# K of eight tiles in one run a partition, products of their own for the memory keys, and another order of the opening

## The chip, the cores and the metric

The kernel runs on one core of a Trainium2 chip. The metric is the device time of one execution in microseconds (us). The engines are TensorE (PE; its weight load is listed as PEld), VectorE (DVE), ScalarE (ACT), GpSimd (POOL) and SyncE (SP); each works through its own list of instructions in order and waits there for semaphores of the others. SP only issues transfers here.

## The reference

Three stages, one after the other, on 4 x 768 = 3072 tokens of 512 features.

```
scores = scale * q_c @ concat(mem_k, k[c-16 : c+32+8])^T   # per head (8) and chunk of 32 queries: 8 + 56 keys
a      = exp(scores - max);  a = a / (sum(a) + 1e-9)
x      = a @ concat(mem_v, v[c-16 : c+32+8])
y      = softplus(x @ w_in) @ w_out                         # 512 -> 2048 -> 512
z      = leaky(y @ w_in2, alpha) @ w_out2                   # max(h,0) + alpha*min(h,0), 512 -> 2048 -> 512
```

## The kernel before, in words

Tokens are taken in 24 tiles of 128 (`QT`), four to a block of 512 (`TB`, six blocks). One tile's attention is a fixed row of pieces. SP loads q (2 transfers), K (`load_k`, one) and v (`load_v`, six). ACT puts q in order (`a_order`, two halves), POOL copies the eight memory keys beside both ends of K (`a_mem`), so that every chunk's 64 keys stand in one piece. PE makes the scores (`a_scores`: 16 products of 64 columns, called s0, s1, ... below), DVE takes the maximum (`a_max`), subtracts it (`a_shift`), ACT takes exp, DVE sums (`a_sum`) and inverts (`a_norm`), POOL (tiles 0 to 7) or DVE (later tiles) multiplies by the inverse (`a_share`), PE transposes (t0, t1, ...), ACT copies out (`a_turned`), PE multiplies with v (`a_values`: x0, x1, ...), ACT and DVE split the result into a high and a low part (`a_high`, `a_low`). The trace calls the buffers qk, v, ps_s, nm, sm, r, ps_t, pt, ps_x and x; later tiles keep q, K and the shares in qt, kt and s_sb.

The first MLP runs in 96 steps (`steps`, from `SEGMENTS`): step i makes one 128-wide slice of the hidden layer for one block in 12 products of 512 columns (h0, h1, ...; PSUM ps_hh), ACT takes softplus and the high part g, DVE the low part of g, and 12 more products (o0, o1, ...) add it to four output banks ps_o. Blocks 0 and 1 take turns: four slices each, four each, eight each; blocks 2 to 5 then take 16 slices in one go. At such a change of segment (o4, o8, o12, o16, ...) ACT and DVE must first copy the four banks out (o_sb). The weights come as 64-bit words ("raw", 0.5 MB each); DVE turns each into 32 bits with five instructions ("word"), ACT makes the high part and POOL the low part ("wsplit"). The second MLP (ps_q) follows.

The order on every engine is not written by hand. `schedule` gives each piece an engine, an estimated duration, the pieces it follows and a due time made of the step's time and a number from the table `O`; `Plan.run` takes, whenever an engine is free, the able piece with the earliest due time. Eight rounds feed the steps' times back, and the plan with the earliest end is issued piece by piece. All instructions pass one helper, so the trace has them all on line L71, and views go by buffer names. Where the plan sees PE idle, `keep_busy` sets products on a zeroed buffer ("zero") ahead of a piece. The first eight tiles keep q, K and v in rooms of the weight pool; tile 8 and the later ones have rooms of their own.

Of the kernel before, what the change touches and what calls it, by code (L numbers as in the profile page):

```python
# [13 lines left out]
B, H, S, D = 4, 8, 768, 64  # L14
# [68 lines left out]
RUNS = 8  # L83
O = {'qo': 19.43, 'km': 103.61, 's': 132.4, 'm': 86.98, 'c': -51.87, 'e': 175.6, 'n': -19.49, 'r': -46.35, 'w': -19.52, 't': 95.77, 'pt': 85.42, 'v': 4.11, 'xh': -85.13, 'xl': -37.52, 'first': 4.43, 'gap': 13.49, 'second': 13.8, 'gap2': 10.89, 'raw': 76.14, 'ab': -97.97, 'cl': -24.77, 'ca': -41.63, 'cb': -28.14, 'cc': -52.39, 'wh': 1.69, 'wl': -37.29, 'odd': 61.8, 'sp': 29.0, 'hi': -84.66, 'lo': 120.66, 'out': 14.22, 'wait': 0.06, 'sloads': 10.35, 'qo0': 31.77, 'qo1': 59.63, 'km0': 45.44, 'km1': -1.09, 's0': 33.53, 's1': 68.06, 'm0': 99.26, 'm1': -29.86, 'c0': 87.42, 'c1': 86.99, 'e0': -47.46, 'e1': 46.23, 'n0': 20.17, 'n1': -4.91, 'r0': 23.19, 'r1': -6.49, 'w0': -81.15, 'w1': -23.28, 't0': 107.79, 't1': -40.96, 'pt0': 0.74, 'pt1': -5.53, 'v0': -87.68, 'v1': 71.52, 'xh0': -18.53, 'xh1': -22.32, 'xl0': 2.53, 'xl1': 34.49, 'by0': 3.34, 'by1': 1.01, 'va': -80.0, 'vb': -248.8, 'vc': -188.24, 'vd': -121.62, 'ra': -92.44, 'rb': -99.39, 'rc': -59.46, 'wld': -3.93, 'dra': -16.84, 'qpd': -4.87, 'ca0': 0.43, 'ca1': -2.85}


class Plan:
# [16 lines left out]
    def run(self):  # L104
# [10 lines left out]
        while left:  # L115
# [61 lines left out]
def attention_mlp_mlp_kernel(ctx: ExitStack, tc, qk, v, w1, w2, consts, out):  # L177
# [178 lines left out]

    def load_v(t):
        for u, to, at, n in (
            (0, 0, MEM0, NMEM), (0, NMEM, 0, KW - NMEM), (0, KW, CHUNK, KW),
            (1, 0, 0, KW), (1, KW, SW - KW + NMEM, KW - NMEM), (1, 2 * KW - NMEM, MEM0 - D, NMEM),  # L360
        ):
            part = slice(u * DM, (u + 1) * DM)
            sp.dma_start(out=v_t[t][to:to + n, part], in_=v[t][at:at + n, part])

# [18 lines left out]
    def a_scores(t):  # L383

        ps = score_ps[t] = (ps_acc.tile([P, NPAIR, 2, KW], F32, tag="acc", name="ps_s") if t < TB
                            else ps_a.tile([P, NPAIR, 2, KW], F32, tag="pa", name="ps_s"))
        keep_busy(("s", t), ps.rearrange("p g u k -> p (g u k)"))
        for g in range(NPAIR):
            for j in range(NC):
                u, c = divmod(j, 2)  # L390
                n = 2 * (u * NPAIR + g)
                pe.matmul(
                    ps[c * D:(c + 1) * D, g, u, :], lhsT=q_t[t][:, c, n:n + 2, :].rearrange("p e k -> p (e k)"),
                    rhs=k_t[t][:, g, KEYS[j]:KEYS[j] + KW], start=True, stop=True,
                )

# [22 lines left out]

    def a_shifted_exp(t):  # L420
        _, s, nm, _ = st[t]
        x = score_ps.pop(t).rearrange("p g u k -> p (g u) k")
        for n in range(SLOTS):
            act.activation(out=s[:, n, :], in_=x[:, n, :], func=AF.Exp, bias=nm[:, n, :], scale=1.0 / float(D) ** 0.5)

# [481 lines left out]
    def schedule(when):  # L907
# [7 lines left out]

        def dma(name, issue, move, due, work, after=(), take=(), give=(), eng="SP"):
            add(("i",) + name, eng, issue, due, work, after, take)
            add(("x",) + name, "DMA", move, due, nothing, [("i",) + name])
            add(name, "", 2.0, due, nothing, [("x",) + name], [], give)

        for n, k in enumerate(order):
            f = k // 2
            need = when[first_use[f]] + (O["odd"] if k % 2 else 0)
            dma(("raw", n), 0.45, 1.9, (O["ra"], O["rb"], O["rc"])[n] if n < 3 else need - O["raw"], lambda k=k: load_raw(0, k), [("i", "raw", n - 1)] if n else [("i", "qk", TB - 1, 2)], ["raw"])
            add(("ab", n), "DVE", 0.45, need - O["ab"], lambda k=k: magnitude(0, k), [("raw", n)] + ([("ab", n - 1)] if n else []), ["word"])
# [9 lines left out]
        for i, (b, f, first, final) in enumerate(steps):  # L935
# [30 lines left out]
        def tile(t, prev, due, step=None):  # L966
# [10 lines left out]
            if not start:  # L977
                free_qk += [("s", TB - 1)]
            soon = -100 + 2 * t if start else due - O["sloads"]
            add(("qr", t), "", 0.0, soon, room, free_qk, qrooms)  # L980
# [6 lines left out]
            else:  # L987
                dma(("qk", t, 2), 1.45, 2.7, soon, lambda: (load(), load_k(t)), [("qr", t)])
# [4 lines left out]
            dma(("v", t), 2.9, 2.0, (O["va"], O["vb"], O["vc"], O["vd"])[t] if start else due - 24, lambda: load_v(t), [("vr", t)])  # L993
            queries = [("q", t, c) for c in range(2) if few or c]
# [9 lines left out]
            after_s = [("km", t)] + queries + ([("s", prev)] if prev >= 0 else []) + ([("t", TB - 1)] if t == TB else []) + ([("pt", prev)] if t > 2 * TB else []) + ([("h", step)] if step else [])  # L1004
            if t > 3 * TB:
# [4 lines left out]
            else:  # L1010
                add(("s", t), "PE", 1.2, due - when_due("s"), lambda: a_scores(t), after_s, [] if start else ["pa", "s"] if few else ["pa"], qrooms)
            add(("m", t), "DVE", 0.8, due - when_due("m"), lambda: a_max(t), [("s", t)])
            if not few and O["ca" + "01"[t >= TB]] > 0.5:
                add(("c", t), "DVE", 0.17, due - when_due("c"), lambda: a_bias(t), [("m", t)])
                add(("e", t), "ACT", 1.4, due - when_due("e"), lambda: a_shifted_exp(t), [("c", t)], [], [] if start else ["pa"], table="exp")
# [3 lines left out]
            add(("n", t), "DVE", 0.69, due - when_due("n"), lambda: a_sum(t), [("e", t)])  # L1019
            add(("r", t), "DVE", 0.40, due - when_due("r"), lambda: a_norm(t), [("n", t)])  # L1020
# [160 lines left out]
```

## Time and profile before

| | us |
|---|---|
| three runs | 1087.36, 1089.03, 1088.96 (median 1088.96) |
| the profiled execution, its whole time | 1090.53 |
| its span, first to last instruction | 1088.6 |
| PE busy in it | 1064.7 (98%) |
| DVE busy | 715.6 (66%) |
| ACT busy | 559.0 (51%) |
| POOL busy | 231.2 (21%) |

So PE stands still for some 24 us of the span. The views below tell where, and who holds it up. A row of the timeline gives the start, the duration, the engine, the operation, output<-input, and in brackets the idle time before it with what ended it; a row of the groups ("lines") gives how many, their busy time and the mean of one in ns.

### The profile page before, as it was taken

Reading aid. Unit: us, or ns where it says so; the run is one execution under the profiler, and the core shown is the slowest. Engines: PE = TensorE matmul, PEld = TensorE weight load, DVE = VectorE, ACT = ScalarE, POOL = GpSimd, SP = SyncE. Lnnn points to the kernel's source line nnn. Section 1 sums busy time; section 2 is a strip of 40 time slices with the busy share of each in tenths; the row PEclk is TensorE's granted clock in tenths of the full one; section 3 lists DMA queues with packets and bytes.
Section 4 is the critical chain, followed back from the end, with each engine's and each line's share of the span. In section 5 each row is a group of like instructions: output and inputs, shape, how many; then the busy total and the mean of one; then the engine's idle time right before and its main releaser. Section 6 shows DMA issues by size and latency. Waiting matters only on the chain.

```text
span 1088.6 us, 16448 instructions
## 1 busy us (share of the span) xinstructions
PE 1064.7 (98%) x5999; PEld 873.6 (80%) x6003; DVE 715.6 (66%) x1150; ACT 559.0 (51%) x974; POOL 231.2 (21%) x281
## 2 busy tenths in 40 slices
PE   6789999999999999999999999999999999999998
PEld 4578878888888888888888888888888888888886
DVE  6789989566744554454358156678666779566976
ACT  5654335565553554353244355664555755456643
POOL 4434434334222332223233400000000000000000
PEclk9999999999999999999999999999999999999999
DMA  9955574658644565444356373799874999856904
GB/s 227 226 154 173 170 190 129 172 170 207 173 143 155 158 188 139 171 123 145 107 201 229 132 289 125 283 280 323 199 278 174 329 299 256 251 209 251 377 1 78
DMA packets 173840, 214.55 MB, mean 197 GB/s; under 512 B 96064, under 2 KB 125888, under 8 KB 166848
## 3 DMA queue, kind: packets, MB, share of 16 engines
q1 hardware_dynamic: 169456, 196.59, 56.7%
q0 software_dynamic: 4032, 16.78, 7.8%
q8 instruction: 48, 0.79, 0.3%
q14 instruction: 32, 0.26, 0.1%
q10 hardware_dynamic: 272, 0.13, 0.0%
HBM read 154.74 MB, written 46.14 MB: 185 GB/s over the span
## 4 chain that ended last, share of the span: by engine, by line
PE 91%; DVE 3%; DMA 2%; issue 1%; SPq 1%; ACT 1%; POOL 0%; DVEq 0%; ACTq 0%; POOLq 0%
PE ps_q L71 42%; PE ps_o L71 23%; PE ps_hh L71 22%; DVE word L71 2%; PE ps_x L71 2%; PE ps_s L71 2%; DMA raw<-in_w_dram 1%; PE ps_t L71 1%; DMA qk<-in_qk_dram 1%; SPq L71 1%; DMA v<-in_v_dram 0%; ACT pt L71 0%; DVE sm L71 0%; DVE o_sb L71 0%; DVE g L71 0%
## 5 line engine op out<-in xcount | busy, mean ns | idle before, releaser
L71 PE MATMUL ps_hh<-x,wsplit 128*128 128x512 f32 x1152 | 281.1, 393 | 0.3 <-DVE x L71 0.2
L71 PE MATMUL ps_o<-g,wsplit 128*128 128x512 f32 x1152 | 279.1, 391 | 0.8 <-ACT ta L71 0.7
L71 PEld LDWEIGHTS ps_o<-g,wsplit 128*128 128x128 f32 x1152 | 214.8, 188 | 46.5 <-ACT ta L71 1.1
L71 PEld LDWEIGHTS ps_hh<-x,wsplit 128*128 128x128 f32 x1152 | 215.3, 189 | 45.5 <-DVE x L71 0.5
L71 PE MATMUL ps_q<-g,wout 128*128 128x512 f32 x1008 | 229.3, 389 | 0.0
L71 PE MATMUL ps_q<-xop,win 128*128 128x512 f32 x1008 | 229.1, 389 | 0.0
L71 PEld LDWEIGHTS ps_q<-g,wout 128*128 128x128 f32 x1008 | 189.0, 188 | 39.8 <-ACT gb L71 0.5
L71 PEld LDWEIGHTS ps_q<-xop,win 128*128 128x128 f32 x1008 | 189.2, 188 | 39.3
L71 DVE TENSOR_TENSOR g<-ta,g 128x512 fp32r<-128x512 f32 x96 | 71.2, 742 | 132.0 <-ACT g L71 131.8
L71 ACT CAST g<-gb 128x512 fp32r<-128x512 f32 x168 | 100.9, 622 | 89.6 <-PE ps_q L71 64.2
L71 DVE TENSOR_TENSOR g<-gb,g 128x512 fp32r<-128x512 f32 x168 | 114.0, 686 | 35.5 <-ACT g L71 33.6
L71 ACT CAST g<-ta 128x512 fp32r<-128x512 f32 x96 | 59.6, 621 | 147.5 <-PE ps_o L71 147.3
L71 ACT ACTIVATE ta<-ps_hh 128x512 f32<-128x512 f32 x96 | 57.4, 598 | 106.4 <-PE ps_hh L71 106.0
L71 DVE SCALAR_TENSOR_TENSOR word<-raw,word 128x512 int32<-128x512 int32 x128 | 104.6, 818 | 2.5
L71 ACT ACTIVATE tp<-gb 128x512 f32<-128x512 f32 x48 | 30.4, 633 | 91.8 <-DVE gb L71 91.8
L71 POOL TENSOR_TENSOR wst<-wsum,wst 128x512 fp32r<-128x512 f32 x32 | 42.1, 1316 | 122.4 <-ACT wst L71 122.3
L71 DVE TENSOR_SCALAR word<-word 128x512 f32<-128x512 f32 (+1 forms) x128 | 66.1, 521 | 1.8
L71 POOL DMA_DIRECT2D gb<-gb x12 | 10.5, 872 | 264.2 <-DVE g L71 183.0
L71 POOL TENSOR_TENSOR wsplit<-word,wsplit 128x512 fp32r<-128x512 f32 x32 | 48.9, 1530 | 64.4 <-ACT wsplit L71 64.2
L71 DVE TENSOR_SCALAR word<-raw 128x512 int32<-128x512 int32 x64 | 38.1, 597 | 36.8 <-DMA raw<-in_w_dram 23.8
L71 DVE SCALAR_TENSOR_TENSOR gb<-gb,tp 128x512 f32<-128x512 f32 x48 | 33.2, 691 | 44.0 <-ACT tp L71 44.0
L71 POOL TENSOR_TENSOR wst<-word,wst 128x512 fp32r<-128x512 f32 (+1 forms) x32 | 36.6, 1145 | 113.4 <-ACT wst L71 113.4
(81 smaller groups left out, 926.0 us busy)
## 6 DMA issues: line engine op xcount, KB each, us to landing
wout<-out_ops SPq DMA_DIRECT2D x42, 1024.0 KB
raw<-in_w_dram SPq DMA_DIRECT2D x64, 512.0 KB
win<-in_ops SPq DMA_DIRECT2D x24, 1024.0 KB
win<-in_ops SPq DMA_DIRECT2D x24, 768.0 KB
out_ops<-wst SPq DMA_DIRECT2D x56, 256.0 KB
in_ops<-wst SPq DMA_DIRECT2D x24, 512.0 KB
gb<-gb POOLq DMA_DIRECT2D x12, 1024.0 KB, 13.3
v<-in_v_dram SPq DMA_DIRECT2D x48, 128.0 KB
```

The source lines that it names most:

```text
L71: i = getattr(self.engine, name)(*args, **kw)
```

## The change

K. For the first eight tiles `load_k` writes K as it lies in HBM, 640 numbers (2560 bytes) in one run a partition; before, it wrote four runs of 640 bytes with room for the memory keys between them. `a_mem` is called for tile 8 and later ones only, and `a_scores` makes the first and the last chunk's scores of a tile in two products, 8 memory keys and 56 others (`PARTS`): 24 products a tile in place of 16, with the same columns in all.

Engines. With 'wld' 1 the low part of the first weight half is made by DVE, not POOL. With 'qpd' 1 the second half of q is put in order by DVE, not ACT, for tiles 0 to 3. `load_v` can take ACT's queue, and the exponent can be taken with shift and sum in one; both stay unused ('vq*' and 'ca*' are 0), so all loads stay on SP.

The plan. Estimates change: a DVE piece counts 0.88 of its old duration and 0.3 (was 0.25) of what overlaps POOL; after 90 us a PE piece behind more than 2 us of idle time counts 1.6 us more; transfers land 1.3 us after their bytes have moved (was 2.0); drains that add into DRAM count more. All of the table `O` is new. So every engine has another order.

```
-O = {'qo': 19.43, 'km': 103.61, 's': 132.4, 'm': 86.98, ...
+O = {'qo': 23.95, 'km': 62.18, 's': 86.7, 'm': 107.2, ... 'wld': 1, 'dra': 0, 'qpd': 1, 'ca0': 0, 'ca1': 0, 'vq0': 0, ...
+PARTS = (((0, MEM0, NMEM), (NMEM, 0, KW - NMEM)), ((0, CHUNK, KW),), ((0, 2 * CHUNK, KW),), ((0, KT - KW + NMEM, KW - NMEM), (KW - NMEM, MEM0, NMEM)))
 (Plan.run)
+                if t > 90.0 and t - free.get("PE", 0.0) > 2.0:
+                    us += 1.6
-            if engine == "DVE" and free.get("POOL", 0.0) > t:
-                us += 0.25 * min(us, free["POOL"] - t)
+            if engine == "DVE":
+                us *= 0.88
+                if free.get("POOL", 0.0) > t:
+                    us += 0.3 * min(us, free["POOL"] - t)
 (load_k)
-        sp.dma_start(out=k_t[t][:, :, NMEM:NMEM + KT], in_=qk[t][:, QN:].rearrange("p (g k) -> p g k", k=KT))
+        if t < 2 * TB:
+            sp.dma_start(out=k_t[t].rearrange("p g k -> p (g k)"), in_=qk[t][:, QN:])
+        else:
+            sp.dma_start(out=k_t[t][:, :, NMEM:NMEM + KT], in_=qk[t][:, QN:].rearrange("p (g k) -> p g k", k=KT))
 (a_scores)
-                pe.matmul(
-                    ps[c * D:(c + 1) * D, g, u, :], lhsT=...,
-                    rhs=k_t[t][:, g, KEYS[j]:KEYS[j] + KW], start=True, stop=True,
-                )
+                for to, at, w in PARTS[j] if t < 2 * TB else ((0, KEYS[j], KW),):
+                    pe.matmul(
+                        ps[c * D:(c + 1) * D, g, u, to:to + w], lhsT=...,
+                        rhs=k_t[t][:, g, at:at + w], start=True, stop=True,
+                    )
 (schedule)
-            add(("km", t), "POOL", 0.4, due - when_due("km"), lambda: a_mem(t), [("qk", t, 2)])
+            if few:
+                add(("km", t), "POOL", 0.4, due - when_due("km"), lambda: a_mem(t), [("qk", t, 2)])
-                add(("s", t), "PE", 1.2, ...
+                add(("s", t), "PE", 1.2 if few else 1.45, ...
-            soon = -100 + 2 * t if start else due - O["sloads"]
+            soon = (-500, O["qb"], O["qc"], O["qd"])[t] if start else due - O["sloads"]
```

SP before issues q and K of tiles 0 to 3, then v0, raw0, v1, raw1, v2, raw2, v3, and after that each tile's qk with its v: qk4, v4, qk5, v5, raw3, qk6, v6, raw4, qk7, v7, raw5. SP now: qk0, qk1, qk2, v0, v1, qk3, v2, raw0, v3, raw1, raw2, qk4, qk5, v4, qk6, raw3, qk7, v5, raw4, v6, raw5, v7.

PE in the opening, before: from the transpose of tile 4 (v0_357) to that of tile 5 (v0_418); g and wsplit mark the first o step, and the scores of tiles 6 (v0_483) and 7 (v0_568) stand between.

```order
L71 MATMUL ps_t_642<-cst_87,v0_357 128x128 x4
L71 MATMUL ps_s_656<-qk0_419,v0_483 64x64 x16
L71 MATMUL ps_x_689<-pt_93,v0_357 64x64 x8
L71 MATMUL ps_x_689<-pt_94,v0_357 64x64 x8
L71 MATMUL ps_o_708<-g_629,wsplit_458 128x512 x3
L71 MATMUL ps_o_709<-g_629,wsplit_458 128x512 x3
L71 MATMUL ps_o_710<-g_629,wsplit_458 128x512 x3
L71 MATMUL ps_o_711<-g_629,wsplit_458 128x512 x3
L71 MATMUL ps_s_741<-qk0_484,v0_568 64x64 x16
L71 LDWEIGHTS zero_91
L71 MATMUL ps_t_770<-zero_91 128x512
L71 MATMUL ps_t_770<-cst_87,v0_418 128x128 x4
```

The same place on PE now, from the last product of tile 7's scores; tile 4 is v_405, tile 5 v_467, tile 6 v_588, tile 7 v_625.

```order
L72 MATMUL ps_s<-qk_486,v_625 64x8
L72 MATMUL ps_t<-cst,v_405 128x128 x4
L72 LDWEIGHTS zero
L72 MATMUL ps_t<-zero 128x512
L72 MATMUL ps_t<-cst,v_467 128x128 x4
L72 MATMUL ps_hh<-x,wsplit 128x512 x12
L72 MATMUL ps_x<-pt,v_405 64x64 x16
L72 MATMUL ps_o<-g,wsplit 128x512 x12
L72 MATMUL ps_x<-pt,v_467 64x64 x16
L72 MATMUL ps_t<-cst,v_588 128x128 x4
L72 MATMUL ps_o<-g,wsplit 128x512 x12
L72 MATMUL ps_x<-pt,v_588 64x64 x16
```

All scores of the eight tiles now stand ahead of the transpose of tile 4, and the transpose of tile 5 stands ahead of x4 and of the third h step.

DVE before, where tile 4's scores come in (its room is v_357); word<-raw is the first instruction on the fourth weight word, raw3.

```order
L71 TENSOR_REDUCE nm<-ps_s 128x8
L71 SCALAR_TENSOR_TENSOR word<-raw,word 128x512
L71 TENSOR_TENSOR v_357<-ps_s,nm 128x512
L71 TENSOR_SCALAR word<-raw 128x512
L71 TENSOR_REDUCE sm<-v_357 128x8
L71 TENSOR_SCALAR word<-word 128x512
L71 TENSOR_SCALAR sm<-sm 128x8
L71 RECIPROCAL r<-sm 128x8
```

DVE now, at the same place (tile 4 is v_405, tile 5 v_467).

```order
L72 TENSOR_TENSOR v_405<-ps_s,nm 128x512
L72 MEMSET ps_s 64x4x8
L72 TENSOR_REDUCE nm<-ps_s 128x8
L72 SCALAR_TENSOR_TENSOR word<-raw,word 128x512
L72 TENSOR_TENSOR v_467<-ps_s,nm 128x512
L72 TENSOR_REDUCE sm<-v_405 128x8
L72 TENSOR_SCALAR word<-raw 128x512
L72 TENSOR_REDUCE sm<-v_467 128x8
```

The sum of tile 4 stood behind the first instruction on raw3 and stands ahead of it now.

DVE before, at the change of segment ahead of o8 (the two copies to o_sb).

```order
L71 TENSOR_SCALAR word<-raw 128x512
L71 SCALAR_TENSOR_TENSOR word<-raw,word 128x512
L71 TENSOR_SCALAR word<-word 128x512
L71 SCALAR_TENSOR_TENSOR word<-raw,word 128x512
L71 COPY o_sb<-ps_o 128x512 x2
```

DVE now, around its first change of segment, ahead of o4; nm, s_sb, sm and r are those of tile 8.

```order
L72 SCALAR_TENSOR_TENSOR word<-raw,word 128x512
L72 TENSOR_TENSOR s_sb<-ps_s,nm 128x512
L72 TENSOR_SCALAR word<-word 128x512
L72 TENSOR_TENSOR g<-ta,g 128x512
L72 COPY o_sb<-ps_o 128x512 x2
L72 SCALAR_TENSOR_TENSOR word<-raw,word 128x512
L72 TENSOR_REDUCE sm<-s_sb 128x8
L72 SCALAR_TENSOR_TENSOR word<-raw,word 128x512
L72 TENSOR_SCALAR sm<-sm 128x8
L72 RECIPROCAL r<-sm 128x8
L72 TENSOR_SCALAR word<-raw 128x512
L72 TENSOR_TENSOR s_sb<-s_sb,r 128x512
```

Before, no piece of tile 8 stands on PE or DVE ahead of o16; now tile 8's scores follow h4, its transpose o5, tile 9's scores h10 and its transpose o9, and tile 10's scores o10. On ACT tile 8's exp stands ahead of the first copies to o_sb, with a load of its table before it.

## Rows read from the trace of the kernel before

**Rows 1.** The span by stretch: us, busy time of each engine, clock, DMA share, GB/s.
```profile
0.00:75.00 75.00, 56.09 (x660) 40.59 (x665) 54.49 (x110) 45.32 (x84) 31.81 (x70) 0.95 0.83 206
40.00:60.00 20.00, 14.47 (x137) 11.70 (x136) 15.89 (x34) 12.39 (x23) 6.93 (x11) 0.83 1.07 251
75.00:120.00 45.00, 44.86 (x198) 36.89 (x197) 44.73 (x69) 18.39 (x32) 19.15 (x12) 1.00 0.58 177
120.00:1088.00 968.00, 963.73 (x5143) 796.13 (x5142) 616.40 (x973) 495.30 (x859) 180.23 (x200) 1.00 0.64 197
```

**Rows 2.** PE's waits up to 75 us: total, times, longest.
```profile
PE ps_t L71 <- POOL v L71: 6.7, 4, 2.9
...
PE ps_s L71 <- POOL qk L71: 2.1, 2, 1.6
```

**Rows 3.** PE's timeline between 44 and 76 us.
```profile
44.85 0.94 PE L71 MATMUL ps_t<-cst,v 128*128 128x128 f32 x4 [2.94 <-POOL v L71]
...
55.49 0.58 PE L71 MATMUL ps_t<-zero 128*128 128x512 bf16 x1 [2.13 <-DVE x L71]
...
56.58 4.00 PE L71 MATMUL ps_hh<-x,wsplit 128*128 128x512 f32 x12
...
61.59 0.66 PE L71 MATMUL ps_t<-cst,v 128*128 128x128 f32 x4
...
71.02 3.02 PE L71 MATMUL ps_o<-g,wsplit 128*128 128x512 f32 x12
```

**Rows 4.** DVE's timeline at 41.93 us, and around 132 us.
```profile
41.93 0.43 DVE L71 TENSOR_SCALAR word<-raw 128x512 int32<-128x512 int32 x1 [4.47 <-DMA raw<-in_w_dram]
...
131.83 0.67 DVE L71 TENSOR_TENSOR g<-ta,g 128x512 fp32r<-128x512 f32 x1
132.43 3.49 DVE L71 SCALAR_TENSOR_TENSOR word<-raw,word 128x512 int32<-128x512 int32 x1
```

**Rows 5.** The loads' queue from 5 to 13.5 us: packets, MB, share of 16 engines.
```profile
DMA packets 5108, 2.07 MB, mean 244 GB/s; under 512 B 3252, under 2 KB 5033, under 8 KB 5108
```

**Rows 6.** The same from 15 to 24 us.
```profile
DMA packets 1044, 2.41 MB, mean 268 GB/s; under 512 B 197, under 2 KB 197, under 8 KB 1043
```

**Rows 7.** POOL's timeline, the memory keys of tile 4.
```profile
32.23 0.35 POOL L71 COPY qk<-qk 128x32 f32<-128x32 f32 x2 [3.86 <-DMA qk<-in_qk_dram]
```

**Rows 8.** PE's and PEld's timelines, the scores of tile 2.
```profile
14.95 1.15 PE L71 MATMUL ps_s<-qk,v 128*64 128x64 f32 x32
...
14.95 1.01 PEld L71 LDWEIGHTS ps_s<-qk,v 128*64 128x64 f32 x32 [0.17 <-issue]
```

**Rows 9.** DVE's groups by form from 160 to 230 us, a later tile's pieces.
```profile
L71 DVE TENSOR_TENSOR s_sb<-s_sb,r 128x512 f32<-128x512 f32 x4 | 3.3, 824 | 0.1
L71 DVE TENSOR_SCALAR sm<-sm 128x8 f32<-128x8 f32 x4 | 2.9, 717 | 0.0
L71 DVE TENSOR_REDUCE nm<-ps_s 128x8 f32<-128x512 f32 x4 | 2.8, 689 | 1.4 <-PE ps_s L71 1.4
L71 DVE TENSOR_TENSOR s_sb<-ps_s,nm 128x512 f32<-128x512 f32 x4 | 2.7, 684 | 0.0
L71 DVE TENSOR_REDUCE sm<-s_sb 128x8 f32<-128x512 f32 x4 | 2.7, 683 | 2.0 <-ACT s_sb L71 2.0
L71 DVE TENSOR_TENSOR x<-ps_x,x 128x512 fp32r<-128x512 f32 x3 | 2.0, 684 | 0.0
```

**Rows 10.** PE's timeline, the first o step with its g of Rows 4 behind it.
```profile
136.82 1.07 PE L71 MATMUL ps_o<-g,wsplit 128*128 128x512 f32 x4
```

**Rows 11.** ACT's timeline, the exp of a later tile.
```profile
164.20 1.28 ACT L71 ACT_TABLE_LOAD   x1
165.95 0.63 ACT L71 ACTIVATE s_sb<-s_sb 128x512 f32<-128x512 f32 x1 [0.47 <-DVE s_sb L71]
```

**Rows 12.** The chain that ended last, from 60 to 115 us.
```profile
108.79 0.61 DVE o_sb L71
...
109.54 2.97 PE ps_o L71 x12
```

More of the change, by code (lines that the diff above doesn't have):

```diff
@@ L327, in room_qk @@
             raw_q[t] = room[:, :QN // 2]
-            k_t[t] = room[:, QN:QN + NPAIR * KN].rearrange("p (g k) -> p g k", k=KN)
+            k_t[t] = room[:, QN:QN + NPAIR * KT].rearrange("p (g k) -> p g k", k=KT)
         else:
@@ L355, in room_v, with load_v @@
             v_t[t] = apool.tile([P, 2 * DM], F32, tag="v", name="v", bufs=1)
-    def load_v(t):
+    def load_v(t, queue):
         for u, to, at, n in (
@@ L362, in load_v @@
             part = slice(u * DM, (u + 1) * DM)
-            sp.dma_start(out=v_t[t][to:to + n, part], in_=v[t][at:at + n, part])
+            queue.dma_start(out=v_t[t][to:to + n, part], in_=v[t][at:at + n, part])
     def a_order(t, e, other=False):
@@ L418, in a_bias, with a_shifted_exp @@
         dve.tensor_scalar(out=nm, in0=nm, scalar1=-1.0 / float(D) ** 0.5, scalar2=None, op0=ALU.mult)
-    def a_shifted_exp(t):
-        _, s, nm, _ = st[t]
+    def a_shifted_exp(t, sums=False):
+        _, s, nm, sm = st[t]
         x = score_ps.pop(t).rearrange("p g u k -> p (g u) k")
         for n in range(SLOTS):
-            act.activation(out=s[:, n, :], in_=x[:, n, :], func=AF.Exp, bias=nm[:, n, :], scale=1.0 / float(D) ** 0.5)
+            act.activation(out=s[:, n, :], in_=x[:, n, :], func=AF.Exp, bias=nm[:, n, :], scale=1.0 / float(D) ** 0.5, accum_out=sm[:, n, :] if sums else None)
     def a_exp(t):
@@ L914, in nothing, with dma @@
             pass
-        def dma(name, issue, move, due, work, after=(), take=(), give=(), eng="SP"):
+        def dma(name, issue, move, due, work, after=(), take=(), give=(), eng="SP", land=2.0):
             add(("i",) + name, eng, issue, due, work, after, take)
             add(("x",) + name, "DMA", move, due, nothing, [("i",) + name])
-            add(name, "", 2.0, due, nothing, [("x",) + name], [], give)
+            add(name, "", land, due, nothing, [("x",) + name], [], give)
         for n, k in enumerate(order):
@@ L923, in schedule @@
             need = when[first_use[f]] + (O["odd"] if k % 2 else 0)
-            dma(("raw", n), 0.45, 1.9, (O["ra"], O["rb"], O["rc"])[n] if n < 3 else need - O["raw"], lambda k=k: load_raw(0, k), [("i", "raw", n - 1)] if n else [("i", "qk", TB - 1, 2)], ["raw"])
+            dma(("raw", n), 0.45, 1.75, (O["ra"], O["rb"], O["rc"])[n] if n < 3 else need - O["raw"], lambda k=k: load_raw(0, k), [("i", "raw", n - 1)] if n else [("i", "qk", 0, 2)], ["raw"], land=1.3)
             add(("ab", n), "DVE", 0.45, need - O["ab"], lambda k=k: magnitude(0, k), [("raw", n)] + ([("ab", n - 1)] if n else []), ["word"])
@@ L987, in tile @@
             else:
-                dma(("qk", t, 2), 1.45, 2.7, soon, lambda: (load(), load_k(t)), [("qr", t)])
+                dma(("qk", t, 2), 1.65, 2.2, soon, lambda: (load(), load_k(t)), [("qr", t)], land=1.3)
             kafter = [("i", "q", t, 1)]
@@ L992, in tile @@
             add(("vr", t), "", 0.0, soon + 2, lambda: room_v(t), [("i", "qk", t, 2)] + ([("i", "v", prev)] if prev >= 0 else []), vrooms)
-            dma(("v", t), 2.9, 2.0, (O["va"], O["vb"], O["vc"], O["vd"])[t] if start else due - 24, lambda: load_v(t), [("vr", t)])
+            by_act = not few and O["vq%d" % t] > 0.5
+            dma(("v", t), 2.9, 2.4, (O["va"], O["vb"], O["vc"], O["vd"])[t] if start else due - (24 if few else O["ve"]), lambda: load_v(t, act if by_act else sp), [("vr", t)], eng="ACT" if by_act else "SP", land=2.0 if few else 1.3)
             queries = [("q", t, c) for c in range(2) if few or c]
@@ L1002, in tile @@
                 queries += ["qzero"]
[L1003 to L1004 removed]
+            if few:
+                add(("km", t), "POOL", 0.4, due - when_due("km"), lambda: a_mem(t), [("qk", t, 2)])
+            after_s = [("km", t)] if few else [("qk", t, 2)] + queries + ([("s", prev)] if prev >= 0 else []) + ([("t", TB - 1)] if t == TB else []) + ([("pt", prev)] if t > 2 * TB else []) + ([("h", step)] if step else [])
             if t > 3 * TB:
@@ L1014, in tile @@
                 add(("c", t), "DVE", 0.17, due - when_due("c"), lambda: a_bias(t), [("m", t)])
-                add(("e", t), "ACT", 1.4, due - when_due("e"), lambda: a_shifted_exp(t), [("c", t)], [], [] if start else ["pa"], table="exp")
+                with_sums = O["ca" + "01"[t >= TB]] > 1.5
+                add(("e", t), "ACT", 3.0 if with_sums else 1.65, due - when_due("e"), lambda: a_shifted_exp(t, with_sums), [("c", t)], [], [] if start else ["pa"], table="exp")
             else:
@@ L1018, in tile @@
                 add(("e", t), "ACT", 0.65, due - when_due("e"), lambda: a_exp(t), [("c", t)], table="exp")
-            add(("n", t), "DVE", 0.69, due - when_due("n"), lambda: a_sum(t), [("e", t)])
+            if not few and O["ca" + "01"[t >= TB]] > 1.5:
+                add(("n", t), "", 0.0, due, nothing, [("e", t)])
+            else:
+                add(("n", t), "DVE", 0.69, due - when_due("n"), lambda: a_sum(t), [("e", t)])
             add(("r", t), "DVE", 0.40, due - when_due("r"), lambda: a_norm(t), [("n", t)])
```

10 lines of the change are left out of this document (5 added, 5 removed).

## The prediction

> **What bounds the kernel now.** I read the table of stretches first. Up to 75 us PE is busy for 56.09 us; from 75 to 120 us it is busy 44.86 of 45 us, and from 120 to 1088 us 963.73 of 968 [rows 1]. So 18.9 us are lost in the opening and about 4.4 us in all the rest. This change does not touch the number or the size of the 512-column products, so it can give at most what the opening loses, and it can lose wherever PE runs without a gap now.
>
> The list of PE's waits names the opening's losses: 6.7 us in four waits for POOL's share (the longest 2.9), and 2.1 us in two waits for POOL's copies of the memory keys [rows 2]. PE's timeline puts two of these losses in place: 2.94 us ahead of tile 4's transpose and 2.13 us ahead of tile 5's [rows 3]. Behind each the granted clock is lower, 0.83 on average from 40 to 60 us [rows 1], that is, 1.2 in place of 2.4 GHz for about a third of the stretch; h2 takes 4.00 us there, where 12 such products take 2.97 in the row of the chain [rows 3, 12]. The opening is over when o1 starts at 71.02 [rows 3].
>
> The last view is DVE's share of the stretch behind it: 44.73 of 45 us busy from 75 to 120 us [rows 1], and the chain runs through DVE's words until o_sb at 108.79 releases o8 at 109.54 [rows 12]. There DVE is as full as PE.
>
> **The change part by part.** *K and the queue.* A tile's K is 128 x 2560 bytes, 0.33 MB. With small runs the queue moved 244 GB/s, with rows of 2 and 4 KB 268 [rows 5, 6]: 0.33/0.244 - 0.33/0.268 = 0.12 us a tile, 0.8 us by the seventh. Bounds: 0 (the rates also mix q's 256-byte runs and v) and 0.3 a tile. In the new order qk7 is issued ahead of v5, v6 and raw4, 1.57 MB, so it lands 1.57/0.244 = 6.4 us earlier; v7 lands behind one more raw, 2.1 us later, some 55 us in place of 54, and x7 is needed only just before 71. raw3 has one more qk (0.59 MB) and one less v (0.52) ahead of it: 0.3 us later by order, 0.8 earlier by runs, so 0.5 earlier.
>
> The Trainium skill, DMA: Bandwidth & Descriptors, Specifications, gives 512 bytes as the smallest transfer that reaches line rate. By it the runs of 640 bytes lose nothing already, and the 0.12 us are those of q alone. The two rows cannot separate q from K, so this stands as a rival below.
>
> *The memory keys.* POOL's two copies take 0.35 us a tile [rows 7] and go. Behind them K's landing still holds the scores, so of the 2.1 us of waits for them [rows 2] I take a third, 0.7. The extra eight products: a tile's 16 products are 32 passes in 1.15 us, 36 ns each, and their 32 weight loads take 1.01 [rows 8]. Sixteen more passes cost 0.54 us if each is held by its load, nothing if two narrow ones share the time of a wide one or if PE waits anyway. In the first four tiles it waits for loads and shares; for tiles 4 to 7, which fill PE's row, I take all, 4 x 0.54 = 2.2 us.
>
> *Tile 4's sum.* Before, DVE stood 4.47 us for raw3 until 41.93 [rows 4], and tile 4's sum, queued behind that instruction, held the share and so the transpose: that is PE's 2.94 us. Now the sum stands ahead of raw3, and the scores of tiles 6 and 7 stand ahead of the transpose. I take the whole wait: 2.9. Tile 5's transpose stood behind x4, whose room DVE had to free; it now stands ahead of x4 and h2: 2.1. Without these two waits the clock has no reason to fall: h2 gives back 4.00 - 2.97 = 1.0, and what runs behind the first wait (t4 at 0.94 us, a full-clock one at 0.66 [rows 3]) about as much, 1.1 by the same length. What is late next is the share of tiles 6 and 7 on POOL and the weight words of h3.
>
> *Moves onto DVE.* Four q copies and one low part of 512 columns, some 0.68 us each by the nearest row [rows 9], 3.4 us. DVE is busy 54.5 of the first 75 us [rows 1], so most lies in its waits for loads; I take half as late, 1.7, from bounds of 0 and 3.4.
>
> The opening's sum: 0.7 + 2.9 + 2.1 + 2.1 (clock) - 2.2 - 1.7 = 3.9, and with raw3's 0.5 split between PE and DVE 4.2 us. Bounds: 0.7 (only the copies count) and 8.
>
> *Behind the opening.* Ahead of o12 DVE now has the pieces of tile 8, of tile 9 up to the share, and of tile 10 the maximum and the shift. A tile's pieces are 0.689 + 0.684 + 0.683 + 0.717 + 0.824 + 0.684 = 4.3 us by their means [rows 9]; their records overlap by some 0.08 each, and the inverse comes on top: 3.9. So 3.9 + 3.2 + 1.3 = 8.4 us. PE gets three scores, two transposes and one product with v: 4 x 1.15 + 2 x 0.66 = 5.9 us [rows 3, 8]. DVE thus falls back by 2.5 us, and PE arrives 4.2 us earlier while raw3 gives DVE 0.5: 6.2 us short, in a stretch with 0.3 us free. What can give: an ordinary o step has its low part ready at 132.50 for 136.82 [rows 4, 10], 4.3 us early. 6.2 - 4.3 = 1.9 us reach PE. On ACT, tile 8's exp and its table load (1.28 + 0.63 [rows 11]) stand ahead of the copies that release o4: between 0 and 1.9, I take 0.6. The drains that release o8 and o12 stand behind words as o8's did: 0.5 for both. Given back: 3.0 us. Moving these tiles out of the later stretch returns nothing, since PE loses only 4.4 us in 968 there.
>
> Sum: -4.2 + 3.0 = -1.2 us. The profiled execution took 1090.53 us, 1.9 more than its span; by its own time the changed kernel would take 1089.3. That execution lies 1.6 above the median of the runs, 1088.96, and against the median I forecast **1087.8 us**, within 0.2% (2.2 us), which is about what a measurement of this kernel can tell from no change.
>
> **The rivals.** *A: nothing is given back.* The words for a slice have slack that the rows show only at o13, and tiles 8 to 10 could lie in it whole. For it: an o step is served 4.3 us early. Against it: o8's wait behind DVE. Then 1088.96 - 4.2 = 1084.8.
>
> *B: DVE becomes the bound from o4 on.* At a change of segment no slack exists: the banks are drained by DVE behind its words, as at 108.79 [rows 12]. If the 6.2 us show there in full, with the 1.1 of ACT and drains, 7.3 are given back: 1088.96 - 4.2 + 7.3 = 1092.1. It decides from 6.4 us of PE waits behind 75 us (4.2 + 2.2). For it: a word that met POOL took 3.49 us [rows 4] where its kind costs 0.7, and shares and low parts of the pulled tiles run beside POOL too. Against it: the same collision is already paid in the 44.73 us.
>
> The Trainium skill, SBUF — State Buffer, Who interferes with whom, says that a DVE instruction with two SBUF inputs is blocked for the whole of a GpSimd instruction that reads SBUF and came first. The row of the share with both inputs in SBUF, 824 ns against 684 for the shift that reads PSUM [rows 9], agrees in sign. By the rule each share and low part could stretch as the word of 3.49 us did, which would be B.
>
> *C: K's long runs save nothing*, as the rule on DMA has it. Then raw3 and the K of tiles 4 to 7 land 0.8 us later than I take: 1088.6. For it: the faster stretch of the queue held few short runs of any kind, 197 packets of 1044 under 512 bytes [rows 6], so q alone could make the difference.
>
> **How the numbers follow.** The forecast 0.38, A 0.33, B 0.20, C 0.09. The forecast's own range is 1086.2 to 1089.6, from half of the 0.7 to 1.9 us terms. Of the forecast's share 0.03 lies below 1086.8 and 0.02 above 1091.1. Faster: 0.33 + 0.03 = 0.36; slower: 0.20 + 0.02 = 0.22; within 0.2%: 0.42. The range takes in A and B up to its price: 1083.9 to 1092.1; the opening's outer bound (a gain of 8 with nothing returned, 1081) is left out.
>
> **What the profile would show.** No PE wait for POOL's qk before tile 8. Tile 4's transpose directly behind tile 7's scores, with under 1 us of idle time, and h2 at some 3 us at full clock. x7 some 4 us earlier than now. A tile's 24 products in 1.5 to 1.7 us. Between 80 and 150 us PE waits of 2 to 4 us, at o4, at tile 8's transpose, at o10 to o12, put down to ACT's o_sb or to DVE; none would make A right, over 6.4 us B. I would be wrong in the opening if qk4 to qk7 land no earlier or if DVE, with q copies in front of its sums, holds the first four shares; and wrong behind it if POOL, not DVE, is the engine that PE waits for.

## The result, and the profile after

| | before | after |
|---|---|---|
| median (lowest to highest) of six runs on the same chip | 1089.01 (1087.36 to 1091.25) | 1095.41 (1093.19 to 1098.05) |
| ratio, 95% interval | | 1.0056 [1.0037, 1.0076] |
| profiled execution, whole time | 1090.53 | 1094.38 |
| its span | 1088.6 | 1092.2 |

The change makes the kernel slower by 0.56%, some 6 us. The forecast was 1087.8 in a range up to 1092.1: sign and size were wrong. The two profiled executions lie 1.5 above and 1.0 below their medians, so they show 3.85 us of the 6.4 between the medians.

The table of stretches of the changed kernel, columns as in [rows 1]:

```profile
0.00:75.00 75.00, 59.64 (x776) 45.84 (x780) 57.13 (x116) 44.93 (x82) 28.31 (x54) 0.89 0.79 207
75.00:120.00 45.00, 44.23 (x277) 35.96 (x276) 44.68 (x72) 22.63 (x38) 19.81 (x14) 1.00 0.65 196
```

PE is busy 3.5 us longer in the opening than in [rows 1], so its idle time there did fall, from 18.9 to 15.4 us, but with more work and less clock (0.89 for 0.95): the idle time was exchanged for busy time. PE's waits up to 80 us, the answer to [rows 2]:

```profile
PE ps_x L72 <- ACT pt L72: 3.5, 1, 3.5
PE ps_t L72 <- ACT pt L72: 2.8, 1, 2.8
PE ps_t L72 <- DMA cst<-in_consts_dram: 1.9, 1, 1.9
PE ps_t L72 <- POOL v L72: 1.9, 3, 1.1
PE ps_s L72 <- DMA qk<-in_qk_dram: 1.9, 2, 1.5
```

The 6.7 us of waits for POOL's share are down to 1.9 and those for POOL's copies are gone, as forecast. In their place stand three that [rows 2] does not show: 3.5 us at x2, 2.8 at tile 5's transpose, 1.9 for the constants. Waits of the first kind were there before, four short ones at the products with v; now one is long. The line of before:

```profile
PE ps_x L71 <- ACT pt L71: 3.3, 4, 1.7
```

PE's timeline of the changed kernel at the place of [rows 3]:

```profile
47.02 1.59 PE L72 MATMUL ps_s<-qk,v 128*64 128x8 f32 x48 [0.40 <-DMA qk<-in_qk_dram]
49.66 0.66 PE L72 MATMUL ps_t<-cst,v 128*128 128x128 f32 x4 [1.05 <-POOL v L72]
53.13 0.58 PE L72 MATMUL ps_t<-zero 128*128 128x512 bf16 x1 [2.81 <-ACT pt L72]
53.51 1.06 PE L72 MATMUL ps_t<-cst,v 128*128 128x128 f32 x4
54.22 5.25 PE L72 MATMUL ps_hh<-x,wsplit 128*128 128x512 f32 x12
...
73.38 2.79 PE L72 MATMUL ps_o<-g,wsplit 128*128 128x512 f32 x11
```

A tile's 24 products take 1.59 us, and h2 behind the wait takes 5.25 where it took 4.00. The last row is o2. The same products stand ahead of it as stand before ahead of h4, which started at 73.87, behind o1. At that place the changed kernel is 0.5 us early, not 4.2.

Behind it, PE's waits from 80 us to the end, and the longest of them in PE's timeline:

```profile
PE ps_o L72 <- DVE g L72: 1.9, 1, 1.9
PE ps_t L72 <- DVE s_sb L72: 1.7, 2, 0.9
PE ps_hh L72 <- ACT ta L72: 0.3, 1, 0.3
```

```profile
92.10 0.63 PE L72 MATMUL ps_t<-cst,s_sb 128*128 128x128 f32 x4 [0.77 <-DVE s_sb L72]
...
144.38 2.79 PE L72 MATMUL ps_o<-g,wsplit 128*128 128x512 f32 x11 [1.87 <-DVE g L72]
```

The row at 92.10 is tile 8's transpose; it stands behind o4 (88.42), not behind o5. From the end of the opening to the end of the span it is 1088.6 - 73.87 = 1014.7 us before and 1092.2 - 73.38 = 1018.8 now: 4.1 us longer. DVE's timeline says why o12 waits for its g:

```profile
137.79 1.15 DVE L72 TENSOR_SCALAR word<-word 128x512 f32<-128x512 f32 x1
138.87 1.27 DVE L72 COPY o_sb<-ps_o 128x512 f32<-128x512 f32 x2
140.06 0.15 DVE L72 TENSOR_SCALAR sm<-sm 128x8 f32<-128x8 f32 x1
140.25 0.20 DVE L72 RECIPROCAL r<-sm 128x8 f32<-128x8 f32 x1
140.38 0.46 DVE L72 TENSOR_SCALAR word<-word 128x512 int32<-128x512 int32 x1
140.75 0.68 DVE L72 TENSOR_TENSOR s_sb<-s_sb,r 128x512 f32<-128x512 f32 x1
...
143.65 0.68 DVE L72 TENSOR_TENSOR g<-ta,g 128x512 fp32r<-128x512 f32 x1
```

DVE works without a gap through drains, words, and a pulled tile's inverse and share; the low part of g ends at 144.33, and PE goes on at 144.38. In the kernel before, the nearest g was ready 4.3 us early [rows 4, 10].

### The profile page after: what moved, and what is told of

The parts are those of the page before. It is cut to its first block, busy times and chain, and to the rows that moved or that the text cites. A ratio compares the mean times of both kernels' runs of the same rounds, so it can differ in the third digit from the quotient of the medians.

```text
span 1092.2 us, 16594 instructions
## 1 busy us (share of the span) xinstructions
PE 1068.7 (98%) x6113; PEld 878.5 (80%) x6116; DVE 718.4 (66%) x1155; ACT 559.4 (51%) x972; POOL 229.8 (21%) x264
## 4 chain that ended last, share of the span: by engine, by line
PE 86%; DVE 7%; DMA 3%; SPq 2%; issue 1%; ACT 1%; DVEq 0%; ACTq 0%
PE ps_q L72 42%; PE ps_o L72 21%; PE ps_hh L72 20%; DVE word L72 5%; DMA qk<-in_qk_dram 2%; SPq L72 2%; PE ps_x L72 2%; PE ps_s L72 1%; DMA raw<-in_w_dram 1%; PE ps_t L72 1%; DVE g L72 1%; DVE sm L72 0%; DVE o_sb L72 0%; DVE s_sb L72 0%; ACT pt L72 0%
## 5 line engine op out<-in xcount | busy, mean ns | idle before, releaser
L72 DVE TENSOR_TENSOR g<-ta,g 128x512 fp32r<-128x512 f32 x96 | 77.2, 804 | 159.4 <-ACT g L72 159.2
L72 DVE SCALAR_TENSOR_TENSOR word<-raw,word 128x512 int32<-128x512 int32 x128 | 102.0, 797 | 2.7
L72 DVE TENSOR_SCALAR word<-word 128x512 int32<-128x512 int32 (+1 forms) x128 | 66.2, 520 | 1.8
```

Of the source, the lines that this page charges most:

```text
L72: i = getattr(self.engine, name)(*args, **kw)
```

## The experiments

Each ran five rounds beside the kernel before on the same chip; the ratio is to that one. "Behind" is the span less the start of o2 (or the same place). The edits are shown shortened.

**K alone, on the kernel before.** K as one run a partition and 24 products, the old order, the copies gone.

```
-            k_t[t] = room[...KN]       +            k_t[t] = room[...KT]
+        if t < 2 * TB: return          (a_mem)
```

> The kernel before with its own plan and order, and of the change only K in one run a partition, 24 products a tile, and no memory-key copies for the first eight tiles. Theory P (the products cost): a tile's scores took 1.59 us after against 1.15, 0.44 more, 3.5 us in all; less the 2.1 us of waits for POOL's copies at most, so 1 to 2.5 us slower than before, 1090 to 1091.5. Rival Q (the long runs pay): qk rows land 0.1 to 0.3 us earlier each, the products lie in waits, 1 to 2 us faster, 1087 to 1088. If neither term counts: within 0.7 us of before.

Measured: 1.0016 [1.0005, 1.0027]. In its profile PE is busy 57.88 us up to 75, 1.8 more than in [rows 1], o1 starts at 72.61 instead of 71.02, and behind is 1090.2 - 75.46 = 1014.7 as before. So K with its products costs 1.7 us (0.5 to 2.9 by the interval), in the opening.

**K in four runs, in the changed kernel.**

```
-sp.dma_start(out=k_t[t].rearrange("p g k -> p (g k)"), in_=qk[t][:, QN:])
+sp.dma_start(out=k_t[t], in_=qk[t][:, QN:].rearrange("p (g k) -> p g k", k=KT))
```

> The changed kernel with its order and its 24 products, but K written in four runs of 640 bytes again. If the long runs pay, the queue's time a MB rises, raw0 lands later than 26.3 us and the kernel is 1 to 2 us slower than the changed one (1096 to 1097.5). If in the new order the loads are held by SyncE, which waits for earlier transfers to land before it issues the next (11.8 us of such waits up to 60 us after, 6.8 before), the run length decides nothing: the same within 0.7 us.

Measured: 1.0054 [1.004, 1.0068] against 1.0056: the length of the runs does not show in the kernel's time, as rival C has it. In the transfers it does show: a packet of 640 bytes of K took 46.6 ns in this trace in the mean, so four took 186 ns, and one of 2560 bytes took 153.5 in that of the changed kernel (medians 33 and 121 ns). The rule of the Trainium skill, DMA: Bandwidth & Descriptors, Specifications (line rate from 512 bytes on) agrees with the time and not quite with the packets: what the long runs save does not reach the end.

**Copies and 16 products back, in the changed order.** K in four runs; POOL's two copies stand right ahead of each tile's scores.

```
-for to, at, w in PARTS[j] if ...      +for to, at, w in ((0, KEYS[j], KW),):
-lambda: a_scores(t)                   +lambda: (a_mem(t), a_scores(t))
```

> The changed kernel's order with the memory keys as before: POOL's copies ahead of each of the first eight tiles' scores, 16 products a tile, K in four runs. Against the changed kernel (24 products, a tile's scores 1.59 us and not 1.15) PE has 3.5 us less to do; eight copies of 0.35 us come back on POOL. Theory P: PE waits for loads and shares in the opening either way, so only what stands in PE's full row pays: 1 to 2.5 us faster than the changed kernel. Rival Q: POOL's copies stand ahead of the shares in its queue and wait for K, so nothing is gained or it is slower.

Measured: 1.0067 [1.0053, 1.008], no faster than the change. PE waits for the copies, which on POOL mostly wait for K's landing:

```profile
PE ps_s L72 <- POOL qk L72: 8.7, 5, 3.2
```

**Four pieces of the opening, one at a time, in the changed order.** Each takes away what a wait of the list above was put down to: tile 3's shift ahead of the first word instruction on raw0; the constants ahead of v0; the inverses of tiles 4 and 5 right behind their sums and the softplus of h1 ahead of tile 6's exp; raw3 ahead of v4.

```
+moved(("ab", 0), after=("c", 3))                       # shift first
+moved(load cst, ahead of load v0)                      # constants first
+moved(("r", 4), after=("n", 4)); moved(("r", 5), after=("n", 5)); moved(("sp", 1), ahead of ("e", 6))
+moved(load raw3, ahead of load v4)
```

> The changed kernel, with one DVE instruction moved: the first one on raw0 stands behind tile 3's shift, not ahead of it. Theory O (order): in the changed kernel DVE stood 3.4 us for raw0 with tile 3's shift behind it, ACT's exp of tile 3 waited for that, and the copies of tile 2's transpose behind that exp, which PE's x2 waited 3.5 us for. Then x2's wait falls under 0.5 us, the clock stays up there, and the kernel gains 2 to 3.5 us (1092 to 1093.5). Rival L (loads): what ends the opening is the landing of raw0 and qk4, which this does not move; x2's wait goes, h0 or s4 waits in its place, and the gain is under 0.7 us.

> The changed kernel, with the constants' load ahead of v0's six loads on SyncE, not behind. Tile 0's transpose waited 1.9 us for it, and the clock was at 1.2 GHz behind that wait (s2 2.77 us, a full-clock one 1.59). Theory O: that wait falls under 0.5 us, s2 takes 1.6 us, and the kernel gains 1 to 3 us. Rival L: the next pieces wait for q3, v and raw0 all the same, and the gain is under 0.7 us.

> The changed kernel with three pieces moved: on DVE the inverses of tiles 4 and 5 stand right behind their sums, not behind the words of raw3; on ACT the softplus of h1 stands ahead of tile 6's exp, so that two table loads go and the copies of tile 4's transpose come 1.5 us earlier. PE's waits ahead of t4 and t5 (1.05 and 2.81 us) and the half-clock h2 (5.25 us) should shrink by 2 to 4 us. Theory D (DVE sets the end of the stretch: in five runs o12's last 11 products began 100.3 to 100.6 us after the first instruction on raw3): raw3 is not moved, so o12's wait grows by what the opening gains and the total is the same within 1 us. Rival P (PE's waits add up): 2 to 4 us faster than the changed kernel.

> The changed kernel with one transfer moved: raw3 is issued ahead of v4, not behind qk6. It should land 3 to 6 us earlier than 43.8. Theory D: o12's wait of 1.9 us and those for tile 8's and 9's shares (1.7) go, 2 to 3.5 us faster than the changed kernel, with o12 still some 100.5 us behind raw3 or no longer waiting. Rival P: K and v of tiles 4 to 7 land 2.3 us later, PE waits longer in the opening and nothing is gained (within 0.7 us, or slower).

Measured: 1.0048 [1.0035, 1.0061], 1.0041 [1.0028, 1.0055], 1.0033 [1.0019, 1.0047] and 1.0042 [1.0027, 1.0056]. All four intervals meet that of the change; at most the third, 0.2% lower, is a gain. In the first three the wait that was aimed at is gone or shorter, and another stands for it. In the fourth it is not: raw3's first word comes at 44.70, now behind other work of DVE and no longer behind its load, and the waits that it was to remove, 1.9 us at o12 and 1.8 for tiles' shares, stand as they were. With the shift first, x2 waits 0.33 in place of 3.53 us, and then the next transpose waits:

```profile
24.78 1.46 PE L72 MATMUL ps_x<-pt,v 128*64 128x64 f32 x32 [0.33 <-ACT pt L72]
...
30.58 1.11 PE L72 MATMUL ps_t<-cst,v 128*128 128x128 f32 x4 [4.02 <-POOL v L72]
```

**Two raws earlier.** raw0 ahead of K of tile 3, raw3 ahead of v4.

```
+moved(load raw0, ahead of load qk3); moved(load raw3, ahead of load v4)
```

> The changed kernel with two transfers moved on SyncE: raw0 ahead of qk3 and v2, raw3 ahead of v4 and qk6. The words of raw0 to raw2 should start some 4 us earlier (22 in place of 26), those of raw3 at 40 in place of 44. Theory S (late words are what the new order of the loads costs): x2's wait of 3.5 us and the waits at t8 and o12 (2.6 us) shrink, 3 to 6 us faster than the changed kernel, at before's level. Rival: qk3 and the later q and K land 2 to 4 us later in exchange, PE waits for them, and the gain is under 1 us.

Measured: 1.0041 [1.0028, 1.0053], not told apart from the change. PE now waits for K's loads: 8.2 us in three waits, up to 4.4, where the changed kernel has 1.9. o2 starts at 71.37, 2.0 earlier, and 0.8 of it is lost again behind (1091.0 - 71.37 = 1019.6). raw3's first word comes at 41.14, 2.6 us earlier than in the changed kernel, and yet PE's waits behind 74 us stay:

```profile
PE ps_t L72 <- DVE s_sb L72: 1.8, 2, 0.9
PE ps_o L72 <- DVE g L72: 1.6, 2, 1.4
```

**Tile 4's sum first, in the kernel before.** This is the step that the prediction booked at 2.9 us, alone.

```
+moved(("r", 4), after=("n", 4)); moved(("ab", 3), after=("r", 4))
```

> The kernel before, with one thing of the new order: on DVE tile 4's sum and inverse stand ahead of the first instruction on raw3. In before that instruction stood 4.47 us for its load, and PE's t4 waited 2.94 us for tile 4's share. If the prediction's step holds (the whole wait goes and the clock stays up behind it), 2.9 us of wait and about 1.1 us of clock go: 2 to 4 us faster than before. If another piece is late next (qk6, s6, tile 5's chain, which stands where it did), t5 or s6 waits in its place: within 0.7 us of before.

Measured: 0.9992 [0.9982, 1.0002]. PE's timeline of this kernel:

```profile
40.05 1.43 PE L71 MATMUL ps_s<-qk,v 128*64 128x64 f32 x32 [2.24 <-POOL qk L71]
41.41 4.31 PE L71 MATMUL ps_hh<-x,wsplit 128*128 128x512 f32 x12
45.56 0.60 PE L71 MATMUL ps_t<-cst,v 128*128 128x128 f32 x4
...
53.88 1.59 PE L71 MATMUL ps_s<-qk,v 128*64 128x64 f32 x32 [1.91 <-POOL qk L71]
```

The 2.94 us ahead of tile 4's transpose [rows 3] are gone, and the scores of tiles 5 and 7 wait 2.2 and 1.9 us for POOL's copies, which wait for K. o1 starts at 70.57 instead of 71.02. Part of this is the execution and not the move: the copy for tile 5 starts at 39.78 here and at 37.52 in the profile of before, and the moved pieces run only from 40.65 on. But the profile of before has the same limit at tile 7, in POOL's timeline:

```profile
51.37 0.45 POOL L71 COPY qk<-qk 128x32 f32<-128x32 f32 x2 [5.78 <-DMA qk<-in_qk_dram]
```

The scores of tile 7 start there at 52.20. Whatever is won ahead of them, they could start some 0.4 us earlier and no more.

**The clamps left out.** In the first MLP the weights' words are not limited to the range of 32 bits: one DVE instruction of five less for each word, 0.4 us. First in the changed kernel, then in the kernel before.

```
-lambda k=k: clamp(0, k, dve)          +nothing
```

> The changed kernel in its own order, without the clamp of the first MLP's weight words (it leaves out one of the five DVE instructions a word, 32 of 0.42 us, some 0.35 us each in the row, and with it the guard against very small and very large weights). Theory D: DVE has 9 us less from raw3 to o12, the waits for DVE at tile 8's and 9's transposes and at o12 go (3.6 us), 2.5 to 4 us faster than the changed kernel. Rival P: what is lost is lost up to 53 us; the opening's waits stay and the gain is under 1 us.

> The kernel before in its own order, without the clamp of the first MLP's weight words (the same thing left out as in the changed kernel without clamp, which came out 0.6% faster than the changed one). Theory D, as a claim on the change (its stretch behind the opening is bound by DVE, and that of before is not): before loses only 1.0 us of PE waits behind 75 us, so it gains under 1.5 us, while the changed kernel gained some 6. Rival C (the clamp costs both kernels alike, in the opening too): it gains 4 us or more as well, and the clamp tells nothing about the change.

Measured: 0.9994 [0.9983, 1.0005] for the changed kernel, 0.62% under the change itself, and 0.9981 [0.997, 0.9993] for the kernel before. The same relief of DVE is worth 6.7 us in the new order and 2.1 in the old. In the changed kernel the waits behind 78 us fall from 3.9 to 1.7, and behind goes from 1018.8 to 1089.8 - 73.49 = 1016.3, while the opening ends where it did. The profiles show 2.8 of the 6.7 us: this one lies 1.9 above its median, that of the changed kernel 1.0 below.

**Tiles 8 to 10 sixteen steps later.** Steps are h and o steps of PE's list, so it is eight slices: tile 8's scores stand at 123.80, behind o10, instead of 79.04; the expectation's o13 is wrong. This is still among the turns of blocks 0 and 1, and its transpose still stands ahead of o12.

```
+if of_tile(piece) and place < stop: place = min(place + 16, stop)
```

> The changed kernel with the attention of tiles 8, 9 and 10 put 16 steps of PE's list later (tile 8's scores behind o13 in place of h5), the rest of the order kept. Theory D: without their 8 us of DVE work ahead of o12 PE waits there no more and runs without a gap from 54 to 145 us; 2.5 to 4 us faster than the changed kernel. Rival P: as little as the no-clamp kernel, and the tiles' work is only moved: within 1 us.

Measured: 1.0069 [1.0053, 1.0085], slower still. Waits behind 78 us:

```profile
PE ps_o L72 <- DVE g L72: 2.2, 2, 1.2
PE ps_s L72 <- POOL kt L72: 1.9, 1, 1.9
PE ps_hh L72 <- ACT ta L72: 1.6, 1, 1.6
```

Behind is 1097.8 - 74.56 = 1023.2. PE's timeline has tile 8's scores and the first wait behind 78 us:

```profile
123.80 1.15 PE L72 MATMUL ps_s<-kt,qt 128*64 128x64 f32 x32
...
134.94 3.02 PE L72 MATMUL ps_hh<-x,wsplit 128*128 128x512 f32 x12 [1.60 <-ACT ta L72]
```

So the stretch that the tiles left has no wait, and waits came with the place they went to, o12 among them. The run moved the tiles; it did not take them away from the turns.

**The two orders spliced at o1.** Both have K in one run and 24 products. One has the old order up to and with o1 and the new one behind, the other the reverse.

```
+cut = names.index(("out", 1)) + 1
+plan.order = opening.order[:cut] + [x for x in behind.order if x[3] not in early_names]
```

> Up to and with o1 every engine has the order of the kernel before, and behind it, for all that is left, that of the changed kernel; K in one run and 24 products a tile are in. Its opening is that of the kernel before with K changed, which ended 1.6 us late and had raw3's first word at about 42. Theory 'the order behind the opening costs 4 us by itself': 1.0016 + 0.0037 = 1.005, the span less the end of the opening about 1018.8. Rival 'the late words of the changed opening (raw3 at 43.8 instead of 41.9) make the waits behind it': 1.0016 to 1.0025, the span less the end of the opening 1015 to 1016, and PE waits of under 1.5 us behind 78 us.

> The other way round: the changed kernel's order up to and with o1, that of the kernel before for all that is left. Theory 'the order behind costs 4 us by itself': span less the end of the opening 1015, and the ratio is 1.0056 - 0.0037 = 1.002. Rival 'the late words of the changed opening cost them': 1.005 to 1.006 and waits of 2 to 4 us behind 78 us. Between them (1.003 to 1.004): the words that are late and the tiles that are pulled make the waits only together. In either case the changed opening has no gain over that of the kernel before with K changed if this comes out at 1.0016 or more.

Measured: old opening, new order behind, 1.0056 [1.0044, 1.0068]; new opening, old order behind, 1.0031 [1.0021, 1.0042]. The list of PE's waits from 76 us on, of the first and then of the second:

```profile
PE ps_o L72 <- DVE g L72: 1.9, 1, 1.9
PE ps_t L72 <- DVE s_sb L72: 1.8, 2, 0.9
...
```

```profile
PE ps_o L72 <- ACT ta L72: 0.7, 1, 0.7
PE ps_hh L72 <- ACT x L72: 0.7, 1, 0.7
PE ps_hh L72 <- DVE x L72: 0.2, 1, 0.2
```

Behind is about 1021.1 in the first (1094.4 - 73.3) and about 1015.7 in the second (1090.8 - 75.1). The waits for DVE's g and s_sb go with the order behind o1, not with the opening. In the second kernel raw3's first word comes at 44.33, later than in the changed kernel (43.78), and yet none of these waits is there, as they stayed when raw3 came early: the rival that the opening's late words make them falls. With 1.0016 for K alone, the order behind costs 0.40% on the old opening (1.0056 - 1.0016) and 0.25% on the new one (1.0056 - 1.0031); the order of the opening costs 0.15% with the old order behind (1.0031 - 1.0016) and nothing with the new. Each of these differences is uncertain by 0.15 to 0.23% (from the intervals of its two ratios). So the order behind costs time in both, in the second only just, the order of the opening is not told from nothing, and whether the two simply add is not shown. A gain of the size that was forecast, 0.4% or more, both exclude.

No kernel here that computes all of the reference is measurably faster than the one before; the best, tile 4's sum first, is the same within its interval.

## Why the prediction was wrong

By the ratios: K with its products +1.7 us (0.16%), the order behind o1 +2.7 to +4.4, the order of the opening 0 to +1.6, each uncertain by 1 to 2.5 us; in all +6.1. The forecast had -4.2 for the opening, products included, and +3.0 behind. Its products and copies are +1.5 of that (2.2 - 0.7), so it had the order of the opening gain 5.7.

*The failed step: "Now the sum stands ahead of raw3 ... I take the whole wait: 2.9", with the 2.1 of tile 5 and the 2.1 of clock that hang on it.* These 7.1 us are not there. I priced each wait by its length and named what is late next without giving it a time. Even the step itself was half done: the new order moves tile 4's sum, but its inverse still stands behind raw3's words, in DVE's timeline:

```profile
43.78 0.68 DVE L72 TENSOR_SCALAR word<-raw 128x512 int32<-128x512 int32 x1 [1.68 <-DMA raw<-in_w_dram]
44.38 0.67 DVE L72 TENSOR_REDUCE sm<-v 128x8 f32<-128x512 f32 x1
...
47.15 0.68 DVE L72 SCALAR_TENSOR_TENSOR word<-raw,word 128x512 int32<-128x512 int32 x1
47.75 0.17 DVE L72 TENSOR_SCALAR sm<-sm 128x8 f32<-128x8 f32 x1
47.95 0.20 DVE L72 RECIPROCAL r<-sm 128x8 f32<-128x8 f32 x1
```

The sum at 44.38 is tile 5's, the inverse at 47.95 tile 4's. Done whole in the kernel before, with sum and inverse ahead of raw3, it removes the wait and brings 0.08% [-0.02, 0.18], 0.9 us: in that order tile 7's scores stand behind it, and their K leaves 0.4 us. In the changed kernel, where that K is early, tile 4's transpose still waits 1.05 us. For tile 5 I saw that the transpose no longer stands behind x4, but not that it now waits for ACT's pt, which ACT issues behind an exp and a softplus: 2.81 us where 2.13 went. The clock did not come back: 0.89 up to 75 us, with waits of 1.9 to 3.5 us still there.

*Loads.* qk7 came early as forecast: tile 7's scores start at 47.02 with 0.4 us of wait, where they start at 52.20 before. But raw3 came at 43.78, 1.9 later than [rows 4] and not 0.5 earlier, and raw0's first word at 26.26 instead of 18.09. My rate of 244 GB/s was that of a full queue. The stretches of the changed kernel from 10 to 20 us, all engines, clock, DMA share and GB/s, and under them SP's waits up to 60 us:

```profile
10.00:15.00 5.00, 2.82 (x54) 2.28 (x56) 3.90 (x9) 1.39 (x3) 2.10 (x5) 0.97 0.68 170
15.00:20.00 5.00, 4.84 (x87) 4.21 (x85) 1.67 (x4) 2.70 (x7) 1.04 (x1) 0.69 0.72 210
```

```profile
SPq L72 <- DMA qk<-in_qk_dram: 7.2, 13, 1.0
SPq L72 <- DMA raw<-in_w_dram: 4.6, 4, 1.7
```

Before, the same two stretches moved 256 and 270 GB/s, and SP's two waits were 4.1 us (6 times) and 2.7. The other profiles agree: in the nine more that have the new order of these loads the two stretches moved 169 to 222 and 164 to 212 GB/s, in the four more with the old one 227 to 263 and 239 to 250. In both programs the loads take eight semaphores in turn, so each waits on SP for the eighth one before it. The new order sets the many small transfers of q, K and v in a row and the large raws late: eight of them hold little, and the engines run dry. That the fill of the queue and not the number of bytes sets these 5 us is read from these rows; no run isolated it.

*Products.* 0.44 us a tile (1.59 against 1.15 [rows 8]) where 0.54 was the bound: right. 8 x 0.44 = 3.5 us are PE's to do, and K alone, with the copies gone, costs 1.7 in time where 1.5 was forecast: that about half of them are hidden in waits held. Which tiles hide theirs no run says.

*Moves onto DVE.* Its busy time up to 75 us rose by 2.6 us, inside the bounds of 0 to 3.4; what of it is in the time no run isolated.

*Behind the opening.* 3.0 us were booked; the splices say 2.7 and 4.4. The place and the engine were right: 3.0 us of PE waits between 80 and 150 us, at tile 8's transpose and at o12, 2.6 of them put down to DVE; o4 did not wait. The clamps' removal shows that DVE's load carries it. Idle time is 3.2 of the 4.1 us (8.2 against 5.0); in the other 0.9 PE is counted busy, and what they are is open. That the 3.0 agree with the splices is in part luck: they were 1.9 for DVE's lag on a PE 4.2 us early, which it was not, and 1.1 for ACT and the drains, of which 0.3 us of a wait for ACT show. So of rival B the mechanism held, but not its point: it needed over 6.4 us of waits here, and 3.9 came. The collision with POOL that B counted on shows at some low parts of g (1.77 us at 85.96, while POOL works from 85.83 to 87.18), and not at o12, where the share at 140.75 and the low part at 143.65 took 0.68 each. The time left its range on the opening's side. (Its other edge, 1083.9, follows from no term; A's price is 1084.8.) Open too is what makes the opening of one and the same order end between 71.4 and 75.0 us in the profiles of its variants, and with it where in 0 to 1.6 us its new order lies.

## What to carry to other kernels

A wait that is removed pays only up to the next thing that is late at that place: before booking it, find for that instruction and the few behind it when each of their other inputs arrives. In a pipeline fill where loads, DVE, POOL and ACT are all some 2 us from being last, single moves change the name of the wait and little else. To judge a rewritten order, splice the old and the new at one point, both ways: two runs said more than six moves of single pieces. And look where a moved piece came to stand before reading its time.

## What was not expected of the hardware

A product of 8 columns next to one of 56 is not free: splitting 8 of a tile's 16 products, with the same columns in all, took 0.44 us more, 55 ns for each split. The columns of a product are thus not its whole price: sixteen products of 64 columns take 1.15 us in [rows 8], and the same columns in twenty-four take 1.59 at 47.02 above.

The clock after a wait differs between executions of the same stretch. At o12 the changed kernel waits 1.87 us and its next eleven products take 2.79 us at a granted clock of 1.00. With the old opening ahead of the same order the wait is 1.88, and the row of PE's timeline and that of the stretch behind it read:

```profile
144.91 4.29 PE L72 MATMUL ps_o<-g,wsplit 128*128 128x512 f32 x11 [1.88 <-DVE g L72]
```

```profile
145.00:150.00 5.00, 5.00 (x15) 0.66 1.03 228
```

The clock fell from 2.4 to 1.2 GHz for part of the stretch, 1.5 us more for the same wait. So a wait of 2 us here cost 2 us in one execution and 3.5 in another; what decides it no run shows.
